# Sixteen copies of value sums issued from ACT's queue, in a windowed attention with two feed-forward layers

## The chip, the cores and the metric

One NeuronCore of a Trainium2 chip runs the whole program in one launch. The metric is the device time in microseconds of that core. Its engines are TensorE (PE, matmuls), VectorE (DVE), ScalarE (ACT), GpSimd (POOL) and SyncE (SP, which only issues DMAs here). Each works through its own instructions in order; semaphores tie them together.

## The reference

Inputs and output are float32. There are 2 batches, 8 heads, 768 positions and a head dimension of 64. The mean of v over 32 positions, `v_sum`, is what the copies in question carry.

```
k_sum = k.reshape(B, H, nb, 32, D).max(axis=3)          # nb = 24 blocks of 32 positions
v_sum = v.reshape(B, H, nb, 32, D).mean(axis=3)
scores_l = scale * q @ k^T, kept where |i - j| < 16, else -1e9
scores_s = scale * q @ k_sum^T + log(32)
a = softmax(concat[scores_l, scores_s])
x = a @ concat[v, v_sum]                                # to 1536 tokens x 512
x = relu(x @ w_in)**2 @ w_out                           # 512 -> 2048 -> 512
h = x @ w2_in; solu = h * softmax(h); out = layernorm(solu) * g_ln @ w2_out
```

## The kernel before

The 1536 tokens are cut into four pieces t of 512, 256, 256 and 512 tokens, each inside one batch. A unit u is one piece and one pair of heads hp (h and h + 4), so there are 16 units, four to a piece. A unit's queries are worked on in blocks of 64, and each block meets 96 positions of k and v, the window of all its queries, and the 24 block sums of its batch, 120 rows in all.

The values of a unit lie in one of three tiles `vw`, 120 rows x 8 blocks x 128 columns (two heads of 64); unit u uses tile u mod 3. `load_v` (lines 258 to 273) fills rows 0 to 95 from memory. Rows 96 to 119 are the 24 sums, the same for every block of the unit. They are made once for each batch and pair of heads: `load_vst` loads v into a tile `kl`, `sum_v0` adds on POOL or DVE, `sum_v1` multiplies with a selector on TensorE, and `sum_v2` copies the result from PSUM to the tile `vs` of the batch, on ACT six times and on DVE twice. `place_vs` (lines 275 to 279) copies them from `vs` to the tile `vw` with one DMA for a unit, repeated over the unit's 8 or 4 blocks: 96 KB for a unit of 512 tokens, 48 KB for one of 256.

The whole order is written out by hand in `ORDER` (lines 21 to 59), a list of steps with a letter, a number and at times an engine (a ACT, d DVE, p POOL); every engine's instructions stand in the order in which the steps emit them. The letters that matter here: lk, lq, lv, ls, l are loads (k, q, v, v for the sums, weights), all issued by SP; k, K and q, Q transpose k and q and copy them from PSUM; y, j, J are the three steps of the sums and P is `place_vs`. For the attention S is scores, R the mask and maximum on DVE, E the exponential on ACT (four activations and four reads), n and N the normalization, T the transposition, C its copy to SBUF (`pt`), V the product with the tile `vw`, H and X the split of its result into a high and a low part on ACT and DVE. a to e, F and f turn the 8-byte weights that were loaded into float32 pairs, a and many F on ACT. M, U, G, D, O are the first feed-forward layer: matmul, relu, two squares on ACT, the low part, and the second matmul. The later layer is emitted after the list.

The stretches of the list around four of the copies:

```
... n6 j3 lk6 k10 K10a k11 K11d N6p l4 J3a P3 m4 F1a f1p T6 m5 lv4 E7 n7 N7p F2a S4 R8 C6a a3 b3 ...
... f5p V5 lv7 H5 P6 Q8d j5 J5d l8 lq10 a6 a7 X5 G1 ls6 T10 C10a lv8 b6 ...
... O8 G9 a13 l14 a14 c12 d12 E19 U10d R20 D9d G10 M11 n19 e12 P12 lv13 P13 N19p U11d lv14 E20 V12 n20 H12 N20p P14 R21 E21 ...
... H14 X14 G13 D13p l16 E23 O12 P15 G14 M15 e14 O13 n23 l17 D14d O14 ...
```

SP issues only DMAs, so its order is the order of the l and P steps, and it stops at each until what that transfer needs is there.

Of the kernel before, what the change touches and what calls it, by code (L numbers as in the profile page):

```python
# [62 lines left out]
def attn_moe_kernel(ctx, tc, q, k, v, w_in, w_out, w2_in, w2_out, g_ln, out):  # L63
    nc = tc.nc
# [4 lines left out]
    P = 128  # L69
# [4 lines left out]
    NSUM = S // 32  # L74
    WK = 96
    WN = WK + NSUM
# [82 lines left out]
    NVB = 3  # L159
    vw = [ap.tile([WN, NBLK, P], F32, name=f"vw{i}") for i in range(NVB)]  # L160
# [114 lines left out]
    def place_vs(u):  # L275
        t, hp = units[u]
        for b, s0, b0, nb in segs[t]:
            src = vs[b][32 * hp:32 * hp + NSUM]
            nc.sync.dma_start(out=vw[u % NVB][WK:WN, b0:b0 + nb], in_=src.unsqueeze(1).to_broadcast([NSUM, nb, P]))

    def prep_kw(u, eng):

# [401 lines left out]
    def load_g(n):  # L684
# [7 lines left out]
        "k": lambda n: prep_k0(n // 2, n % 2), "K": lambda n, e: prep_k1(n // 2, n % 2, COPY[e]), "m": prep_ks,  # L692
        "q": prep_q0, "Q": lambda u, e: prep_q1(u, COPY[e]), "w": lambda u, e: prep_kw(u, COPY[e]),
        "y": lambda i, e: sum_v0(i, ENG[e]), "j": sum_v1, "J": lambda i, e: sum_v2(i, COPY[e]), "P": place_vs,

        "S": att_s, "R": att_r, "E": att_e, "n": att_n0, "N": lambda g, e: att_n(g, ENG[e]), "T": att_t,
# [62 lines left out]
```

## Time and profile before

| | |
|---|---|
| three timed runs | 500.70, 501.98, 502.87 us; median 501.98 |
| profiled execution | 504.72 us, its span 503.0 us |
| busy: PE, DVE, ACT, POOL | 473.9 (94%), 339.0 (67%), 247.9 (49%), 116.9 (23%) us |
| copies of the sums | 16, at 25.2 to 147.3 us, 799 to 977 ns of SP's queue each |
| clock granted to TensorE, mean | 0.983 |

The span runs from the first to the last instruction, and the execution's own time has what lies around it. Busy time counts arithmetic only: an issue of a DMA occupies the queue of the engine that issues it, but is not counted as its busy time. In a timeline a line is the start, the duration, the engine, the line of the kernel, the instruction with the tile written and the tiles read, and in brackets how long the engine was idle before it and what ended that.

### The profile page before, as it was taken

Reading aid. Unit: us, or ns where it says so; the run is one execution under the profiler, and the core shown is the slowest. Engines: PE = TensorE matmul, PEld = TensorE weight load, DVE = VectorE, ACT = ScalarE, POOL = GpSimd, SP = SyncE. Lnnn points to the kernel's source line nnn. Section 1 sums busy time; section 2 is a strip of 40 time slices with the busy share of each in tenths; the row PEclk is TensorE's granted clock in tenths of the full one; section 3 lists DMA queues with packets and bytes.
Section 4 is the critical chain, followed back from the end, with each engine's and each line's share of the span. In section 5 each row is a group of like instructions: output and inputs, shape, how many; then the busy total and the mean of one; then the engine's idle time right before and its main releaser. Section 6 shows DMA issues by size and latency. Waiting matters only on the chain.

```text
span 503.0 us, 8088 instructions
## 1 busy us (share of the span) xinstructions
PE 473.9 (94%) x2968; PEld 394.8 (78%) x2968; DVE 339.0 (67%) x756; ACT 247.9 (49%) x576; POOL 116.9 (23%) x134
## 2 busy tenths in 40 slices
PE   3686699999999999999999999999999999999997
PEld 2465477789999888888888888888877888888886
DVE  4777889875785459345237778986778787665560
ACT  3687688777764544435326536465522332222231
POOL 3255432721321331511022302101312112110000
PEclk9788899999999999999999999999999999999999
DMA  9999886486224122333011332330000010000011
GB/s 189 206 233 201 214 206 171 98 156 137 74 60 110 51 83 87 81 94 81 36 43 42 124 124 89 125 125 1 1 1 1 22 42 22 21 22 22 21 43 42
DMA packets 60359, 44.04 MB, mean 88 GB/s; under 512 B 46624, under 2 KB 49184, under 8 KB 60320
## 3 DMA queue, kind: packets, MB, share of 16 engines
q1 hardware_dynamic: 60320, 43.53, 34.9%
q8 instruction: 23, 0.38, 0.3%
q14 instruction: 16, 0.13, 0.1%
HBM read 39.19 MB, written 3.15 MB: 84 GB/s over the span
## 4 chain that ended last, share of the span: by engine, by line
PE 78%; DVE 7%; DMA 4%; issue 4%; POOL 3%; ACT 3%; SPq 2%; POOLq 0%; DVEq 0%; ACTq 0%
PE h L505 25%; PE acc L537 23%; PE po L647 13%; PE h L587 9%; DMA kl<-in_v_dram 2%; PE lt L624 2%; PE at L316 2%; PE at L381 1%; POOL kl L242 1%; DMA qr<-in_q_dram 1%; PE at L361 1%; DVE sm L337 1%; ACT sm L345 1%; DVE wf L444 1%; POOL sm L355 1%
## 5 line engine op out<-in xcount | busy, mean ns | idle before, releaser
L505 PE MATMUL h<-xh,wi 128*128 128x512 f32 (+1 forms) x432 | 131.9, 371 | 0.0
L537 PE MATMUL acc<-gh,wo 128*128 128x512 f32 (+1 forms) x432 | 130.2, 368 | 0.0
L505 PEld LDWEIGHTS h<-xh,wi 128*128 128x128 f32 x432 | 79.3, 190 | 14.5 <-issue 0.8
L537 PEld LDWEIGHTS acc<-gh,wo 128*128 128x128 f32 x432 | 78.7, 188 | 14.3 <-issue 1.0
L505 PE MATMUL h<-xl,wi 128*128 128x512 f32 (+1 forms) x216 | 79.5, 368 | 0.0
L537 PE MATMUL acc<-gl,wo 128*128 128x512 f32 (+1 forms) x216 | 79.2, 367 | 0.2 <-DVE gl L94 0.2
L587 PE MATMUL h<-w,wf 128*128 128x512 f32 x288 | 67.4, 390 | 0.5 <-DVE st L598 0.5
L587 PEld LDWEIGHTS h<-w,wf 128*128 128x128 f32 x288 | 54.0, 188 | 11.9 <-PE lt L624 0.7
L515 ACT ACTIVATE r<-h 128x512 f32<-128x512 f32 (+1 forms) x34 | 19.0, 559 | 63.7 <-PE h L505 62.6
L94 POOL TENSOR_TENSOR gl<-r,gh 128x512 fp32r<-128x512 f32 (+1 forms) x19 | 21.5, 1131 | 117.9 <-ACT r L524 103.4
L523 ACT ACTIVATE gh<-r 128x512 fp32r<-128x512 f32 (+1 forms) x54 | 31.3, 580 | 35.0 <-DVE r L517 26.8
L537 PEld LDWEIGHTS acc<-gl,wo 128*128 128x128 f32 x216 | 40.7, 188 | 7.1 <-DVE gl L94 0.7
L505 PEld LDWEIGHTS h<-xl,wi 128*128 128x128 f32 x216 | 41.0, 190 | 6.3
L94 DVE TENSOR_TENSOR gl<-r,gh 128x512 fp32r<-128x512 f32 (+1 forms) x35 | 25.8, 738 | 23.6 <-ACT r L524 21.8
L597 ACT ACTIVATE st<-h,nm 128x1024 f32<-128x1024 f32 x12 | 13.4, 1117 | 51.1 <-DVE nm L594 51.1
L454 DVE SCALAR_TENSOR_TENSOR wf<-st,wf 128x512 uint32<-128x512 uint32 x48 | 36.5, 763 | 1.0
L345 ACT ACTIVATE sm<-sm,mn 128x120 f32<-128x120 f32 x96 | 36.5, 383 | 0.5 <-DVE mn L337 0.4
L437 ACT ACTIVATE wf<-st 128x512 f32<-128x512 f32 x48 | 31.1, 660 | 8.9 <-DMA st<-in_moe_w_in_dram 6.4
L451 DVE SCALAR_TENSOR_TENSOR wf<-st,wf 128x512 uint32<-128x512 uint32 x48 | 34.3, 718 | 1.1
L524 ACT ACTIVATE r<-r 128x512 f32<-128x512 f32 (+1 forms) x54 | 31.6, 585 | 1.8
L440 DVE TENSOR_SCALAR wf<-wf 128x512 f32<-128x512 f32 x48 | 24.8, 518 | 11.1 <-ACT wf L437 11.0
L610 POOL TENSOR_TENSOR vr<-vr,mhalf 128x1 f32<-128x1 f32 x12 | 6.6, 550 | 105.0 <-DVE vr L609 105.0
(126 smaller groups left out, 755.6 us busy)
## 6 DMA issues: line engine op xcount, KB each, us to landing
st<-in_moe_w_out_dram SPq DMA_DIRECT2D x24, 512.0 KB, 3.4
st<-in_moe_w_in_dram SPq DMA_DIRECT2D x32, 256.0 KB, 4.2
st<-in_moe_w_in_dram SPq DMA_DIRECT2D x8, 512.0 KB, 4.0
kl<-in_v_dram SPq DMA_DIRECT2D x8, 384.0 KB, 4.2
kl<-in_k_dram SPq DMA_DIRECT2D x16, 192.0 KB, 4.5
out_dram<-ob SPq DMA_DIRECT2D x11, 256.0 KB, 2.0
vw<-in_v_dram SPq DMA_DIRECT2D x16, 168.0 KB, 3.9
qr<-in_q_dram SPq DMA_DIRECT2D x16, 128.0 KB, 5.0
```

The lines of the kernel that those rows point to most:

```text
L94: eng.tensor_tensor(out=lo, in0=x, in1=hi.bitcast(F32), op=ALU.subtract)
L345: nc.scalar.activation(out=sm[:, j], in_=sm[:, j], func=AF.Exp, bias=mn[:, j:j + 1], scale=-1.0, accum_out=su[:, j:j + 1])
L437: nc.scalar.activation(out=wf_t[n], in_=st_t[n].rearrange("p (n t) -> p n t", t=2)[:, :, 1], func=AF.Abs)
L440: nc.vector.tensor_scalar(out=wf_t[n], in0=wf_t[n], scalar1=C_LO, scalar2=C_HI, op0=ALU.max, op1=ALU.min)
L451: nc.vector.scalar_tensor_tensor(out=w, in0=st[:, :, 0], scalar=29, in1=w, op0=ALU.logical_shift_right, op1=ALU.bitwise_or)
L454: nc.vector.scalar_tensor_tensor(out=w, in0=st[:, :, 1], scalar=0xC0000000, in1=w, op0=ALU.bitwise_and, op1=ALU.bitwise_or)
L505: nc.tensor.matmul(ps[:, 0:hi - lo], wi[:, wsel, d, :], x[t][:, d, lo:hi], start=(n == 0), stop=(n == 3 * HP - 1))
L523: nc.scalar.activation(out=gh, in_=r, func=AF.Square)
L524: nc.scalar.activation(out=r, in_=r, func=AF.Square)
L537: nc.tensor.matmul(acc_t[e][:, lo:hi], wo[:, wsel, e, :], x, start=(edge(s, -1, 3) and i == 0), stop=(edge(s, 1, 3) and i == 2))
L587: nc.tensor.matmul(h2[:, fs], x[:, c, :], w_t[NW1 + nh * NDC + c][:, wsel, :], start=(n == 0), stop=(n == 3 * NDC - 1))
L647: nc.tensor.matmul(po[:, ds], x[:, cs], w_t[NW1 + 8 + c][:, wsel, ds], start=(n == 0), stop=(n == 3 * NF2 - 1))
```

## The change

The DMAs of `place_vs` are issued by ACT instead of SP. Their sources, destinations and sizes, and the order in which the steps are emitted, stay as they are, so that on ACT a copy stands between the activations of the steps around it.

```diff
     def place_vs(u):
         t, hp = units[u]
         for b, s0, b0, nb in segs[t]:
             src = vs[b][32 * hp:32 * hp + NSUM]
-            nc.sync.dma_start(out=vw[u % NVB][WK:WN, b0:b0 + nb], in_=src.unsqueeze(1).to_broadcast([NSUM, nb, P]))
+            nc.scalar.dma_start(out=vw[u % NVB][WK:WN, b0:b0 + nb], in_=src.unsqueeze(1).to_broadcast([NSUM, nb, P]))
```

## Rows read from the trace of the kernel before

**Rows 1.** Windows: stretch, its length, busy us of each engine (instructions), clock, DMA, GB/s.
```profile
0.00:62.50 62.50, 39.11 (x426) 29.97 (x426) 46.23 (x165) 39.39 (x130) 26.84 (x52) 0.86 1.03 209
62.50:100.00 37.50, 35.92 (x320) 27.96 (x319) 32.37 (x94) 30.92 (x92) 16.55 (x15) 1.00 0.65 161
100.00:150.00 50.00, 49.83 (x556) 45.17 (x554) 36.08 (x130) 36.60 (x123) 14.43 (x15) 1.00 0.50 104
150.00:503.00 353.00, 349.06 (x1671) 291.72 (x1671) 224.32 (x369) 141.02 (x234) 59.08 (x52) 1.00 0.18 56
```
**Rows 2.** Line 279: its instructions, ns min/median/max, first and last start in us.
```profile
L279 SPq DMA_DIRECT2D vw<-vs x16: 799/852/977, 25.2 to 147.3; - x16
```
**Rows 3.** Timeline of SP's queue from 112 us (P12 and the load behind it).
```profile
112.52 0.84 SPq L279 DMA_DIRECT2D vw<-vs  x1
113.42 0.51 SPq L269 DMA_DIRECT2D vw<-in_v_dram  x1
```
**Rows 4.** Timeline of ACT and PE from 129 us (G10's squares, V12).
```profile
129.18 0.42 ACT L523 ACTIVATE gh<-r 128x256 fp32r<-128x256 f32 x1 [0.43 <-PE acc L537]
129.63 0.42 ACT L524 ACTIVATE r<-r 128x256 f32<-128x256 f32 x1
...
130.51 1.15 PE L381 MATMUL at<-pt,vw 120*64 120x64 f32 x32
```
**Rows 5.** The tile vw: all transfers into it, from issue to landing.
```profile
DMA to landing us min/median/max: 2.0/3.8/5.6
```
**Rows 6.** Windows, columns as in rows 1.
```profile
58.00:60.00 2.00, 2.00 (x11) 1.49 (x5) 1.60 (x11) 0.30 (x1) 0.00 (x0) 0.50 0.89 287
125.00:130.70 5.70, 5.70 (x76) 5.24 (x76) 4.45 (x18) 5.21 (x19) 0.44 (x1) 1.00 0.00 1
```
**Rows 7.** Timeline of ACT from 136 us (H13).
```profile
136.72 0.60 ACT L397 ACTIVATE xh<-at 128x512 fp32r<-128x512 f32 x1 [1.87 <-PE at L381]
```
**Rows 8.** Timeline of ACT, DVE and PE from 147.9 us (G14, D14, O14).
```profile
147.94 0.40 ACT L523 ACTIVATE gh<-r 128x256 fp32r<-128x256 f32 x1
...
148.87 0.98 DVE L94 TENSOR_TENSOR gl<-r,gh 128x256 fp32r<-128x256 f32 x1 [0.43 <-ACT r L524]
...
149.91 0.39 PE L537 MATMUL acc<-gl,wo 128*128 128x256 f32 x1 [0.17 <-DVE gl L94]
```
**Rows 9.** Timeline of ACT, DVE and PE from 44 us (K10, F1, b3, scores).
```profile
44.20 0.49 ACT L679 ACTIVATE kT<-at 128x384 f32<-128x384 f32 x1 [2.34 <-PE at L199]
...
45.01 0.63 ACT L679 ACTIVATE wi<-wf 128x512 fp32r<-128x512 f32 x1
...
48.88 0.46 DVE L440 TENSOR_SCALAR wf<-wf 128x512 f32<-128x512 f32 x1 [0.47 <-ACT wf L437]
...
57.14 1.08 PE L316 MATMUL at<-kw,qT 64*64 64x120 f32 x16 [1.94 <-DVE qT L676]
```
**Rows 10.** Timeline of ACT, DVE and PE from 71 us (H5, b6, T11).
```profile
71.43 0.38 ACT L397 ACTIVATE xh<-at 128x256 fp32r<-128x256 f32 x1 [1.29 <-PE at L381]
...
72.47 0.42 DVE L440 TENSOR_SCALAR wf<-wf 128x512 f32<-128x512 f32 x1
...
77.92 0.62 PE L361 MATMUL at<-ident,sm 128*120 128x128 f32 x4 [0.77 <-DVE sm L355]
```
**Rows 11.** Timeline of PE from 38 us (V1, j3).
```profile
38.09 1.15 PE L381 MATMUL acc<-pt,vw 120*64 120x64 f32 x32 [1.02 <-DMA vw<-vs]
...
43.02 0.40 PE L249 MATMUL acc<-kl,sel 96*24 96x128 f32 x2 [2.95 <-POOL kl L242]
```
**Rows 12.** Chain that ended last: start, duration, what (a load of v, M0, M1).
```profile
32.71 6.72 DMA kl<-in_v_dram
...
58.22 4.07 PE h L505 x12
...
63.60 2.99 PE h L505 x12
```
**Rows 13.** Waits of SP's queue: us in total, times, longest.
```profile
SPq L279 <- ACT vs L679: 7.6, 1, 7.6
```

## The prediction

> **What bounds the kernel now.** I read the table by stages first [rows 1]. In the first 62.5 us TensorE is busy for 39.11 us only: it waits there for the attention's operands, the 16 DMA engines are full (share 1.03), and DVE (46.23) and ACT (39.39) are busier than it is. From 62.5 to 100 us TensorE is busy for 35.92 of 37.50, so 1.6 us are still lost to other engines. After that it is the bound itself: 49.83 of 50.00, then 349.06 of 353.00. So a load that comes earlier can pay only in the first stage, while a delay that reaches TensorE's own order after 62.5 us is paid in full, and nothing behind it gives it back.
>
> Next the sixteen copies. Each holds SP's queue for about 0.85 us (799 to 977 ns) [rows 2]. SP runs ahead of the other engines: P12 was issued at 112.52 us, and SP's next issue began at 113.42, when that one had ended [rows 3]; the products V12, which P12 serves, start 18 us later, at 130.51 [rows 4]. ACT has no such lead. It works through its instructions in the written order, and a copy on its queue leaves when ACT gets there. The question for each copy is therefore where in ACT's order it falls, what stands behind it, and when TensorE wants the tile. The transfers themselves stay the same, on the same 16 engines.
>
> **The change part by part.** It removes 16 x 0.85 = 13.6 us of issue from SP and adds them to ACT, as waiting places of the sequencer and not as work of the engine. No instruction is added. No new wait on TensorE appears either: the products that free a tile are followed on ACT by the H of the same unit before the next P of that tile comes up. I walked through ORDER with ACT's timeline beside it and found four copies with no cover.
>
> P12. In the order stand G10, M11, P12, lv13, P13, E20, V12. G10's first square on ACT is released by TensorE at 129.18, its second starts at 129.63 and ends at 130.05 [rows 4]. P12 comes right after, so it leaves between 129.63 and 130.05; I take 129.84. TensorE does M11 meanwhile and wants V12 at 130.51. Transfers into this tile land 2.0 us after issue at the fastest, 3.8 at the median [rows 5]. From 125 to 130.7 us the DMA engines stand still (share 0.00) [rows 6], so I stay near the fast end and take 2.5. 129.84 + 2.5 - 130.51 = **1.8 us** of TensorE standing still (ends: 129.63 + 2.0 gives 1.1; 130.05 + 3.8 gives 3.3). ACT can't come earlier by running ahead: G10 waits for TensorE itself. P13 behind it and P14 delay E20, E21 and the two pt copies by two to three issues, 1.7 to 2.6 us; TensorE is then 1.8 late itself, and ACT's next idle time (1.87 us before 136.72 [rows 7]) takes the rest.
>
> P15. ACT runs without a gap up to G14 at 147.94; its second square releases DVE's gl at 148.87 after 0.43 us of idling, and that releases TensorE at 149.91 after 0.17 [rows 8]. ACT leads this chain, so P15 ahead of G14 is paid. I take **0.75**, one issue less the tail of the read still running (ends 0, if ACT's arithmetic runs beside an issue, and 0.98).
>
> P3. It follows J3a, whose sums it reads, and stands before F1a at 45.01 [rows 9]. Behind it are E7 and a3; DVE sits idle for 0.47 us until a3 is there, at 48.88, and then DVE's run leads up to qT, for which TensorE waits 1.94 us at 57.14 [rows 9]. So the delay reaches the start of the first M0: **0.85** (ends 0, and 1.7 if it also waits for a load of SP's).
>
> P6. ACT's H5 starts at 71.43, after 1.29 us of idling [rows 10], and a6 follows it. P6 comes between. DVE takes a6's output at 72.47, as soon as it is there or nearly so, and leads this stretch: TensorE waits 0.77 us for DVE's sm at 77.92 [rows 10]. One issue less a little slack is **0.7** (ends 0 and 0.98).
>
> The twelve others I cost at **0.2** together. They have ACT's idle time behind them, as P2 the 2.34 us before 44.20 [rows 9], or delay something that is not wanted for some us. If that cover is gone, each costs up to 0.85; I allow 2 in all. P1 leaves later too, and V1 at 38.09 was already waiting for it; but TensorE then idles for 2.95 us until POOL's sums are there at 43.02 [rows 11], so some 2 us of that are covered.
>
> What SP gives back. A long DMA leg of the chain's front is the load of v at 32.71, 6.72 us [rows 12]. It waits for its buffer, not for SP; but P1's 96 KB no longer stand in the queue before it, and 96 KB at 209 GB/s [rows 1] are 0.47 us. I credit **-0.4** (ends 0 and -1.0, since more loads may move up). The longest wait of SP at the copies, 7.6 us for J6a [rows 13], goes too, but in a stage where TensorE is already full.
>
> Sum: 1.8 + 0.75 + 0.85 + 0.7 + 0.2 - 0.4 = **+3.9 us**. The profiled execution took 504.72 us, of which the span is 503.0; it would be 508.6. The three timed runs have their median at 501.98, 2.7 below it, and the terms do not hang on that difference: 501.98 + 3.9 = **505.9 us**.
>
> The granted clock is a term that I leave at zero and keep for the range. It fell to 0.50, the 1.2 GHz level, in 58 to 60 us [rows 6] after the 1.94 us wait at 57.14 in a stretch where TensorE did little; M0 took 4.07 us there, M1 at full clock 2.99 [rows 12]. The stall at V12 is as long, but lies in dense work. If the clock falls there, add about 1.1.
>
> **The rivals.** (1) An issue on ACT costs it next to nothing, since its arithmetic runs on. For it: the records show SP issuing, never ACT. Against: SP's own next issue starts only when the last has ended [rows 3]. P12 still lands late, so +1.1 to 1.8: 503.5 us.
>
> (2) The issues on ACT are dearer than on SP, since both queues issue at once in the front, where SP issues almost without pause. With twice the price for P3, P4, P6 and the small ones (0.85 more at three places, 2 for the twelve) and the clock falling at V12 (1.1): 3.9 + 2.6 + 2 = 8.5, 510.5 us. The Trainium skill speaks for this one (Perfetto Trace Analysis, DMA Instruction — HWDGE): the block that generates descriptors is shared by the issuing sequencers and locked for one at a time, and the profiled issue contains the wait for the lock. By that an ACT copy in the front pays up to one SP issue more; SP being the only one to issue here, no row of before shows such a wait.
>
> (3) Faster: SP's issue is what holds back the front. P0 to P4 cost its queue 5 x 0.85 = 4.25 us in the front; if every load behind them moved up by that and the operands with them, 4.25 us of TensorE's 23.4 idle us there (62.5 - 39.11) [rows 1] would go. Less a stall at V12 at its low end, 1.1, and with ACT's issues hidden: -3.15, 498.8 us. It decides for faster from the point where the front gains over 1.1. Against it: the DMA share is 1.03 there, so an earlier issue mostly waits longer. The same page (DMA Optimizations) advises to spread DMAs over the queues when descriptor generation is the bottleneck; by the DMA share it is not.
>
> (4) The change does nothing that counts: stalls at V12 and credits of the front cancel, 502 us.
>
> **How the numbers follow.** Mine 0.56, with its own range 503.8 to 509; rivals (1) 0.18, (2) 0.14, (3) 0.08, (4) 0.04. What a measurement can tell from no change is some 0.5%, 2.5 us: slower from 504.5 on. Of mine 0.06 lies below that. Slower 0.50 + 0.14 = 0.64; same 0.06 + 0.18 + 0.04 = 0.28; faster 0.08. The range leaves out rival (3) and the far end of (2): 501.5 to 510.
>
> **What would show it.** P12's issue on ACT after 129.6 us counted from the same G10, and a TensorE wait before V12, released by the copy, of 1.1 to 3.3 us; a wait of 0.8 to 1.1 instead of 0.17 at the gl products after P15; M0 starting 0.4 to 1.7 us later than 58.22; a6 and DVE's use of it later by 0.7.  Wrong would be: V12 without a wait, M0 at 58 or earlier, or arithmetic of ACT's that starts beside a running issue of its own.

## The result, and the profile after

The changed kernel takes 508.24 us (four runs, 507.95 to 509.40), the kernel before beside it 501.71 (four runs, 500.70 to 502.87). The ratio is 1.0130, with a 95% interval of 1.0107 to 1.0154: **6.5 us slower, between 5.4 and 7.7**. Measured again on another occasion it was 507.93 against 502.02, a ratio of 1.0116 (1.0069 to 1.0163). The forecast was 505.9, slower, with a range up to 510: the sign and the range hold, the size was 2.3 us short. A ratio is of fast runs alone, so one run further down, 508.66 us with P1 alone on ACT, counts in its kernel's median and not in its ratio.

The profiled execution took 508.02 us. By stages, with the columns of [rows 1]:

```profile
0.00:62.50 62.50, 40.20 (x422) 31.39 (x423) 45.74 (x163) 39.42 (x129) 26.11 (x52) 0.86 0.97 201
62.50:100.00 37.50, 35.31 (x315) 27.14 (x315) 32.56 (x95) 31.16 (x91) 15.38 (x14) 1.00 0.76 188
100.00:150.00 50.00, 48.17 (x539) 43.42 (x538) 34.74 (x127) 34.57 (x113) 13.95 (x16) 1.00 0.37 82
150.00:506.30 356.30, 352.14 (x1697) 294.66 (x1695) 226.15 (x375) 143.71 (x245) 61.73 (x54) 1.00 0.18 57
```

The third stage has lost 1.7 us of TensorE's work and the last one is longer by what came before it. The span grew by 3.3 us only (503.0 to 506.3), half of what the timed runs lost. The trace of before stands about 3 us above its own timed runs, and the first experiment is about that.

**P12 and V12**, the timelines of ACT and PE that answer to [rows 4]:

```profile
130.59 0.42 ACT L523 ACTIVATE gh<-r 128x256 fp32r<-128x256 f32 x1 [0.42 <-PE acc L537]
131.03 0.42 ACT L524 ACTIVATE r<-r 128x256 f32<-128x256 f32 x1
131.04 1.65 ACTq L279 DMA_DIRECT2D vw<-vs  x2
132.74 0.39 ACT L345 ACTIVATE sm<-sm,mn 128x120 f32<-128x120 f32 x1 [1.29 <-DVE r L517]
...
133.81 1.15 PE L381 MATMUL at<-pt,vw 120*64 120x64 f32 x32 [1.83 <-DMA vw<-vs]
```

P12 leaves just behind the start of G10's second square, V12 waits 1.83 us for it; the granted clock stays at 1.00 through this stage. ACTq marks what ACT's sequencer issues.

**P15 and P6, P3.** First the rows that answer to [rows 8], then those to [rows 10], then P3's.

```profile
149.40 0.42 ACT L524 ACTIVATE r<-r 128x256 f32<-128x256 f32 x1
149.44 0.80 ACTq L279 DMA_DIRECT2D vw<-vs  x1
149.73 0.38 ACT L345 ACTIVATE sm<-sm,mn 128x120 f32<-128x120 f32 x1
...
153.22 0.38 PE L537 MATMUL acc<-gl,wo 128*128 128x256 f32 x1 [0.17 <-DVE gl L94]
```
```profile
72.28 0.38 ACT L397 ACTIVATE xh<-at 128x256 fp32r<-128x256 f32 x1 [0.87 <-PE at L381]
72.34 0.79 ACTq L279 DMA_DIRECT2D vw<-vs  x1
73.18 1.26 ACT L437 ACTIVATE wf<-st 128x512 f32<-128x512 f32 x2 [0.51 <-DMA vw<-in_v_dram]
...
73.89 0.43 DVE L440 TENSOR_SCALAR wf<-wf 128x512 f32<-128x512 f32 x1
...
79.34 0.62 PE L361 MATMUL at<-ident,sm 128*120 128x128 f32 x4 [0.92 <-DVE sm L355]
```
```profile
45.47 0.48 ACT L679 ACTIVATE kT<-at 128x384 f32<-128x384 f32 x1
...
46.27 0.80 ACTq L279 DMA_DIRECT2D vw<-vs  x1
47.11 0.63 ACT L679 ACTIVATE wi<-wf 128x512 fp32r<-128x512 f32 x1 [0.87 <-DVE kT L676]
```

P15's issue at 149.44 runs beside E23's activations, which stand before it in ACT's order and were queued already; the wait at the gl products is 0.17 us as before. P6 lets a6 and so DVE's b6 come 0.57 later than H5 does (73.89 against 72.47 is +1.42; H5 is +0.85). P3 lets F1a begin 2.10 later than at 45.01, of which K10 before it brings 1.27 and P3 the other 0.83.

**The front.** PE's long waits, and the first M0 and M1 in the chain (as [rows 9, 11 and 12]):

```profile
34.45 0.62 PE L249 MATMUL acc<-kl,sel 96*24 96x128 f32 x2 [4.49 <-POOL kl L242]
40.97 1.97 PE L381 MATMUL acc<-pt,vw 120*64 120x64 f32 x32 [2.02 <-DMA vw<-vs]
47.58 0.95 PE L361 MATMUL acc<-ident,sm 128*120 128x128 f32 x4 [2.02 <-POOL sm L355]
...
58.05 1.07 PE L316 MATMUL at<-kw,qT 64*64 64x120 f32 x16 [0.51 <-DVE qT L676]
```
```profile
35.95 4.89 DMA vw<-vs
59.12 4.06 PE h L505 x12
64.50 2.95 PE h L505 x12
```

The first two waits are new in size. Before, the same two matmuls waited 0.75 us and 1.02 us [rows 11 has the second]. The first follows from a load on SP's queue, here in the trace after and, below it, in that of before:

```profile
27.63 0.31 SPq L236 DMA_DIRECT2D kl<-in_v_dram  x1
```
```profile
24.62 0.47 SPq L236 DMA_DIRECT2D kl<-in_v_dram  x1
...
32.28 0.40 PE L249 MATMUL acc<-kl,sel 96*24 96x128 f32 x2 [0.75 <-POOL kl L242]
```

The load is ls2, v for the third set of sums. It issues 3 us later although SP has less to do. The waits of SP's queue say why (over the whole run: us in total, times, longest); before, there was no row of a load that waits for a copy:

```profile
SPq L272 <- DMA vw<-vs: 6.5, 3, 2.8
SPq L190 <- DMA vw<-vs: 4.7, 1, 4.7
SPq L236 <- DMA vw<-vs: 4.4, 1, 4.4
SPq L422 <- DMA vw<-vs: 3.0, 1, 3.0
...
```

With two smaller rows these are 20.0 us, but only 8.1 of them lie before 62.5 us: the 4.4 of L236, which is ls2, 2.8 of L272 and 0.9. The 4.7 and the 3.0 come later. ls2 fills a tile `kl` and has no use for the copy's tile. What it shares with P0 is a semaphore. Each DMA reports its landing on one of eight, DMAHW0 to DMAHW7, given out in turn over the DMAs of both queues, and in these programs a DMA does not issue until the last one on its semaphore has landed. In the built programs (engine, number among all DMAs of the program from 0, line, transfer, waits):

```
before, SP    28 L236 DMA kl<-in_v_dram 96x2x512 [waits DMAHW4_49,PE_49]
before, SP    29 L279 DMA vw_106<-vs 24x8x128 [waits DMAHW5_49,Activation_49]
after,  ACT   21 L279 DMA vw_106<-vs 24x8x128 [waits DMAHW5_49]
after,  SP    29 L236 DMA kl<-in_v_dram 96x2x512 [waits DMAHW5_49,PE_49]
```

Before, P0 stood one place behind ls2. After, it stands eight places ahead of ls2 and so has the same semaphore; but ACT gets to it at 22.55 us only, and by the events of the semaphore it lands at 27.56. ls2 leaves at 27.63.

### The profile page after: what moved, and what is told of

Same layout as the page of the kernel before. It is cut to its first block, busy times and chain, and to the rows that moved or that the text cites. A ratio compares the mean times of both kernels' runs of the same rounds, so it can differ in the third digit from the quotient of the medians.

```text
span 506.3 us, 8090 instructions
## 1 busy us (share of the span) xinstructions
PE 475.8 (94%) x2968; PEld 396.6 (78%) x2968; DVE 339.2 (67%) x756; ACT 248.9 (49%) x576; POOL 117.2 (23%) x134
## 4 chain that ended last, share of the span: by engine, by line
PE 80%; DMA 7%; issue 3%; DVE 3%; ACT 3%; POOL 2%; SPq 1%; ACTq 0%; POOLq 0%; DVEq 0%
PE h L505 25%; PE acc L537 24%; PE po L647 13%; PE h L587 9%; DMA kl<-in_k_dram 2%; DMA qr<-in_q_dram 2%; PE lt L624 2%; PE at L316 2%; DMA vw<-vs 1%; PE at L381 1%; PE at L361 1%; PE acc L361 1%; PE acc L381 1%; DMA kl<-in_v_dram 1%; DVE wf L454 1%
## 5 line engine op out<-in xcount | busy, mean ns | idle before, releaser
L440 DVE TENSOR_SCALAR wf<-wf 128x512 f32<-128x512 f32 x48 | 24.9, 520 | 12.0 <-ACT wf L437 11.8
L355 POOL TENSOR_TENSOR sm<-sm,su 128x480 f32<-128x480 f32 x17 | 17.3, 1017 | 61.2 <-DVE su L351 48.3
```

The source lines that it names most:

```text
L440: nc.vector.tensor_scalar(out=wf_t[n], in0=wf_t[n], scalar1=C_LO, scalar2=C_HI, op0=ALU.max, op1=ALU.min)
```

## The experiments

Theory A: what costs is that the copies are late on ACT, for the products that read them (P12, P1) and for SP's loads that share their semaphores (P0). Theory B: what costs is ACT's time of issue, 0.8 us for each copy behind which ACT waits. Two of the twelve runs are of unchanged kernels; in the others the edit is which units' copies ACT issues, as in

```diff
-            nc.scalar.dma_start(out=vw[u % NVB][WK:WN, b0:b0 + nb], ...
+            (nc.scalar if u in (0,) else nc.sync).dma_start(out=vw[u % NVB][WK:WN, b0:b0 + nb], ...
```

and in some a step moved in ORDER. In one table, with the difference from the kernel before (its median was 501.7 to 502.0 beside them) worked out from the ratio:

| copies on ACT | moved | median us | ratio (95%) | us |
|---|---|---|---|---|
| all (the change) | | 508.24 | 1.0130 (1.0107 to 1.0154) | +6.5 |
| all, again | | 507.93 | 1.0116 (1.0069 to 1.0163) | +5.8 |
| all but P12 | | 506.73 | 1.0083 (1.0059 to 1.0106) | +4.2 |
| all | P12 | 504.95 | 1.0068 (1.0042 to 1.0094) | +3.4 |
| all | P0, P1, P12 | 503.59 | 1.0040 (1.0016 to 1.0064) | +2.0 |
| P5 to P15 | | 503.74 | 1.0037 (1.0017 to 1.0057) | +1.9 |
| P5 to P15 | P12 | 501.80 | 0.9999 (0.9975 to 1.0024) | -0.1 |
| P0 to P4 | | 505.38 | 1.0053 (1.0026 to 1.0081) | +2.7 |
| P1 | | 504.58 | 1.0045 (1.0015 to 1.0075) | +2.3 |
| P0 | | 502.99 | 1.0024 (1.0003 to 1.0045) | +1.2 |
| P0 | P0 | 501.37 | 0.9988 (0.9972 to 1.0003) | -0.6 |
| P0, P1 | P0, P1 | 502.04 | 0.9993 (0.9971 to 1.0014) | -0.4 |

**A second trace of the kernel before** (no edit).

> The kernel before, unchanged, for a second trace: its profiled execution took 504.72 us where its timed runs take 501.7, so a part of what the change costs is hidden between the two traces. Expected by both theories: an execution near 501.7 us, some 3 us shorter than the first one in the stretch before 62.5 us, and equal to it from 150 us to the end.

Missed: 505.19 us, and the front is no shorter. The first stage of this trace, and below it that of the kernel with P0 alone on ACT and early, whose profiled execution took 501.28:

```profile
0.00:62.50 62.50, 39.52 (x424) 30.26 (x424) 46.56 (x165) 39.06 (x129) 26.86 (x52) 0.89 1.06 216
```
```profile
0.00:62.50 62.50, 41.51 (x456) 31.68 (x457) 49.00 (x169) 43.03 (x144) 27.93 (x53) 0.97 1.04 210
```

The 71 timed runs of the kernel before beside the experiments took 499.7 to 504.8 us. Both of its profiled executions stand at the upper end or above. The second kernel, whose timed runs agree with before's, shows in its trace how a shorter front looks: 2 us more of TensorE's work done by 62.5 us, and a granted clock of 0.97 instead of 0.86 to 0.89. The traces also show what goes with a long execution. In both traces of before, POOL's three adds for the sums (L242) run beside two steps of DVE (L440, L444), and the two take 2.13 and 2.22 us; in the trace after, the load that the adds wait for comes later, and the two steps, done by then, take 0.85. First before, then after:

```profile
54.34 2.72 POOL L242 TENSOR_TENSOR kl<-kl 96x512 f32<-96x512 f32 x3
54.58 1.30 DVE L440 TENSOR_SCALAR wf<-wf 128x512 f32<-128x512 f32 x1
55.92 0.83 DVE L444 TENSOR_SCALAR wf<-wf 128x512 uint32<-128x512 uint32 x1
```
```profile
56.69 0.42 DVE L440 TENSOR_SCALAR wf<-wf 128x512 f32<-128x512 f32 x1
...
58.37 2.61 POOL L242 TENSOR_TENSOR kl<-kl 96x512 f32<-96x512 f32 x3 [1.88 <-DMA kl<-in_v_dram]
```

Of the fourteen traces of this case seven have the adds beside the steps, which then take 1.9 to 2.2 us together, and seven do not, with 0.8 to 0.9. The first seven executions took 2.5 to 3.4 us more than the median of their kernel's timed runs, the others between 2.2 less and 1.7 more. So before was profiled twice in the long form. How 1.3 us of DVE become some 3, and how many timed runs have this form, is not shown. The front's loss is taken from timed runs, and the trace after against that of before understates it. The waits of ls2 and V1 below lie before 42 us, ahead of this place.

**P12 alone back on SP.** The edit: `u` in all but 12.

> All copies from ACT's queue but P12, which SP issues again. Both theories: the wait of V12 (1.83 us in the trace after, released by ACT's copy, against 0.17 before) goes, and nothing else: 508.2 - 1.8 = 506.4 us. If the time stays at 508.2, something else is late there and takes the wait's place.

Measured 506.73. V12 has no wait in its trace, and 4.2 of the 6.5 us stay.

**The front on SP, and its mirror.** The edits: `u in (5, ..., 15)`, and `u in (0, 1, 2, 3, 4)`.

> P0 to P4 from SP's queue again, P5 to P15 from ACT's. Theory A (in the front a copy from ACT's queue lands late, and SP's loads and the first value products wait for it: ls2 for P0, V1 for P1): of the 6.5 us lost, V12's 1.8 and some 0.5 of P5 and P6 stay, so 504.0 us. Theory B (what costs is ACT's time, 0.8 us for each copy behind which it waits): P0, P1, P2 and P4 stood beside other waits and only P3's 0.85 us comes back, so 507.4 us.

> The mirror: only P0 to P4 from ACT's queue, the rest from SP's. Theory A: the front's 4 us are all here, 505.7 us. Theory B: only P3's 0.85 us, 502.6 us. If this and the kernel with P0 to P4 on SP both stand near the kernel before, the two parts of the loss are not independent.

503.74 and 505.38. The first is theory A's number and 3.7 us below B's. Its trace shows the one loss that is left (ACT, then PE):

```profile
126.30 1.65 ACTq L279 DMA_DIRECT2D vw<-vs  x2
...
129.07 1.15 PE L381 MATMUL at<-pt,vw 120*64 120x64 f32 x32 [1.83 <-DMA vw<-vs]
```

The mirror's median is A's number too; its ratio says +2.7 us (1.3 to 4.1), so B's 0.8 lies outside the interval, and A's 3.9 inside. In its trace ls2 waits as in the kernel after:

```profile
SPq L236 <- DMA vw<-vs: 4.4, 1, 4.4
```

**P0 alone, at its place and early.** The second moves the step: `... K4a P0 N0p ...` instead of `... R2 P0 E2 ...`.

> Only P0 from ACT's queue, all the rest from SP's. Theory A (the load ls2 on SP's queue waits for the completion semaphore that P0's copy holds until it has landed, 27.56 us in the trace after, and issues 3 us late): the wait of the sums' matmul for ls2 grows from 0.75 to some 4 us, of which later waits take back a part, so 504 us (503 to 505.5). Theory B (ACT's time of issue): P0's 1.4 us stand beside PE's waits for other work, 502 us, no difference from before.

> Only P0 from ACT's queue, and emitted right after K4a instead of after R2: ACT issues it several us earlier, so it has landed before ls2 asks for its semaphore; ACT's time of issue is the same. Theory A: ls2 issues near 24.6 again, 502 us, as before. Theory B: ACT's issue costs what it costs in the kernel with P0 alone, whether that is nothing or something; the two agree within 0.7 us.

502.99 and 501.37: +1.2 us (0.2 to 2.3) and -0.6 (-1.4 to 0.2), for the same issue on the same engine. ACT's P0 and SP's ls2 with P0 at its place, then with P0 early:

```profile
22.62 1.43 ACTq L279 DMA_DIRECT2D vw<-vs  x1
...
27.07 0.31 SPq L236 DMA_DIRECT2D kl<-in_v_dram  x1
```
```profile
18.53 1.44 ACTq L279 DMA_DIRECT2D vw<-vs  x1
...
24.95 0.47 SPq L236 DMA_DIRECT2D kl<-in_v_dram  x1
```

In the first, SP's waits have 2.6 us of ls2 for a copy; by the events of their semaphore P0 lands at 27.00, and ls2 leaves at 27.07. With P0 4 us earlier ls2 leaves 2.1 us sooner, near the 24.62 of the kernel before, and no load waits more than 0.6 us for a copy. The place of P0 decides, not its issue alone.

**P12 early, and P0, P1 and P12 early, all on ACT.** The moves: `C17a P12 T18`, `K4a P0 N0p`, `C1a P1 n2`.

> All sixteen copies from ACT's queue, P12 emitted right after C17a, some 5 us earlier on ACT. Both theories: V12's wait of 1.83 us goes and the front is as in the kernel after, 506.4 us. If 0.8 us of issue ahead of Q14's or G9's arithmetic is then on the path, up to 507.2.

> All sixteen from ACT's queue, with P0 emitted after K4a, P1 after C1a and P12 after C17a; as many issues on ACT as in the kernel after. Theory A (the copies' lateness is the loss): 503.3 us, what is left being P5, P6 and a part of P2 to P4. Theory B (the issues' time is the loss): only V12's wait goes, 506.4 us.

504.95 and 503.59. The first is 1.5 below what both expected, and V12 has no wait in its trace; the difference from the kernel after, 2.4 to 3.1 us by the two ratios, holds V12's 1.9 within the intervals. The second is A's number: all sixteen are issued by ACT as in the change, and 3.8 to 4.5 of its 5.8 to 6.5 us are gone. What is left of it, 2.0 us, is put to the front by elimination: P5 to P15 with P12 early cost -0.1 us (below). In the trace ls2 leaves at 26.29 (SP, then PE; V1 at 38.76 has no wait):

```profile
26.29 0.47 SPq L236 DMA_DIRECT2D kl<-in_v_dram  x1
...
34.16 0.40 PE L249 MATMUL acc<-kl,sel 96*24 96x128 f32 x2 [3.16 <-POOL kl L242]
...
38.76 1.15 PE L381 MATMUL acc<-pt,vw 120*64 120x64 f32 x32
```

P0 and P1 early cost nothing when they alone are on ACT (-0.4, below), so the 2.0 us point at P2 to P4, or at all five coming together. P2 to P4 were not timed by themselves; this part stays open.

**The change again.** No edit.

> The changed kernel, unchanged, beside the other three on one chip. All theories: 508.2 us. The kernel with P12 emitted earlier came out at 504.95 where 506.4 was expected; if the changed kernel is itself nearer to 507 here, V12's wait explains that difference alone.

507.93 (505.69 to 510.38), no nearer to 507. The 1.1 us by which the move of P12 gained more than V12's wait are within the intervals and not explained further.

**P1 alone, and P0 and P1 early.** The edits: `u in (1,)`; `u in (0, 1)` with the moves of P0 and P1.

> Only P1 from ACT's queue, at its place (ACT issues it behind K8a and a2, near 36 us, where SP issued it at 31.5). Theory A: V1's wait, 1.0 us in the trace before, grows to some 2 to 4 us and an SP load 8 places behind P1 is held until it has landed; later waits take back a part: 503 us (502 to 504.5). Theory B (ACT's time of issue): 0.8 us beside V1's wait, 501.8 us, no difference from before.

> P0 and P1 from ACT's queue, emitted right after K4a and after C1a, all the rest from SP's. Theory A: both have landed before V0, V1 or a load of SP's asks for them, so V1's wait of 1.0 us goes, and what the next wait takes back of it is open: 501.4 us (500.5 to 502). Theory B: two issues of 1.4 and 0.8 us on ACT where it was busier, 502.5 us. If ls2 or the key loads still wait for a copy, the time is near the one of P0 alone at its old place, 503.

504.58 and 502.04: +2.3 us (0.8 to 3.8) for P1 at its place, theory A's number above the top of its range; nothing (-1.5 to 0.7) for both early. P1's issue on ACT and V1 on PE, with P1 at its place; then with P1 early:

```profile
34.18 1.41 ACTq L279 DMA_DIRECT2D vw<-vs  x1
...
41.15 1.12 PE L381 MATMUL acc<-pt,vw 120*64 120x64 f32 x16 [4.10 <-DMA vw<-vs]
```
```profile
27.30 0.79 ACTq L279 DMA_DIRECT2D vw<-vs  x1
...
36.55 1.15 PE L381 MATMUL acc<-pt,vw 120*64 120x64 f32 x32
```

In the first, the chain has the transfer with 6.83 us, in a front whose DMA engines are full, and 2.7 us of lateness (34.18 against 31.49, when SP issued it) turn into a wait longer by 3.1. With P1 early the wait is gone, but the time is that of the kernel before: the 1.02 us that V1 waited there [rows 11] were no loss. Nor were 2.4 us for which a load of v (L272) waits for a copy in this trace.

**P5 to P15 on ACT, P12 early.** The edit of the front on SP, and `C17a P12 T18`.

> P5 to P15 from ACT's queue, P0 to P4 from SP's, P12 emitted right after C17a. With P12 at its old place this took 503.7 us and its trace showed a loss at V12 alone. Theory A: eleven issues on ACT cost nothing where their copies are in time, 501.8 us. Theory B: some 0.2 us an issue stay, 503 us.

501.80, a ratio of 0.9999. Eleven issues on ACT cost nothing that can be measured here: -0.1 us (-1.3 to 1.2). Nor do the 12.4 us for which SP's loads wait for these copies. V12 has no wait in this trace, with P12 out six us before it:

```profile
123.66 0.79 ACTq L279 DMA_DIRECT2D vw<-vs  x1
...
129.85 1.15 PE L381 MATMUL at<-pt,vw 120*64 120x64 f32 x32
```

By theory B some 1.2 us should have stayed; its 503 lies just inside the interval's end, and A's 501.8 in its middle. The difference to the same kernel with P12 at its old place, 1.9 us, is P12's price by itself.

## Why the prediction came out as it did

Right in sign and inside its range, and one term of it right to a tenth; the rest of its sum was made of the wrong terms. That it fell only 2.3 us short is partly luck: the 2.3 us put on P15, P3 and P6, of which little is to be seen, stood in for a front that was put at next to nothing and cost 2.7 us by itself.

**P12: right.** Forecast +1.8; V12 waits 1.83 us in the trace, and the timed pair with P12 late and early differs by 1.9. The way was right too: ACT could not run ahead of G10, and the copy landed 2.64 us after its issue, where 2.5 was taken. The clock did not fall at that wait.

**P15, forecast +0.75: wrong, no cost is seen.** The end "0, if ACT's arithmetic runs beside an issue" is what came. What waits for an issue is what stands behind the copy in ACT's order. The sequencer reached P15 while E23's four activations were queued ahead of it, and the issue ran beside them. The sign named for a wrong forecast, arithmetic beside a running issue, is in the trace. Where what comes next stands behind the copy, ACT stands still for the whole issue, as at E20, which starts at 132.74 when P12 and P13 have been issued.

**P3, forecast +0.85, and P6, +0.7.** As delays they are there, 0.83 us at F1a and 0.57 at b6. As losses little is to be seen. M0 is 0.90 later (59.12 against 58.22), inside the 0.4 to 1.7 that were asked for, but by chance: F1a was 2.10 us late, 1.27 of it from before P3, and DVE gave 1.28 back on the way, because POOL's adds ran beside its two steps in the trace of before only. So M0's own wait shrank from 1.94 to 0.51, and the 1.94 of [rows 9] belong to the long form of the execution. Past P6, TensorE's lateness against the trace of before grows from 1.27 to 1.42 us. P6 alone was not timed; P5 to P15 without P12's lateness cost -0.1 (-1.3 to 1.2), which leaves it small room.

**The twelve others, forecast 0.2, and SP's relief, -0.4: the step that failed.** They hold P0 and P1, which cost +1.2 and +2.3 us each by itself, and P0 to P4 together +2.7. For P1 the step said that some 2 us of V1's longer wait are covered by the 2.95 us of idling behind it. That wait grew by 3.1 us with P1 alone on ACT, and the cover took up half of it: the sums' matmul behind V1 is 1.5 us late there (44.52 against 43.02). But the transposition after it, which waits for POOL's sm as in the trace after (2.02 us at 47.58), is 3.2 late again (47.76 against 44.60), so the cover did not hold. P0 has no word of its own in the step. V0 does not wait for it; what waited was ls2, a load on SP's queue, by the shared semaphore. So SP's first loads did not move up, as the credit of -0.4 had it, but back: in the front they wait 8.1 us for copies. "The transfers themselves stay the same" was true, and left out that each is also the next one's permission to start.

By timed pieces: 2.7 for P0 to P4 and 1.9 for P12 are 4.6 us of the 5.8 to 6.5. Within the front the pieces do not add up (P0 and P1 by themselves are more than all five, and P2 to P4 were not timed), so how the 2.7 divide among the five is open. The rest, 1 to 2 us, is within the intervals of the pieces and is not settled. The granted clock may hold some of it. The mean granted clock of the changed kernel was 0.982 to 0.983 in all eight runs, that of the kernel before 0.988 on average over the 71 (0.979 to 0.997), and over those 71 runs the time falls by 0.11 us for each 0.001. This would be 0.6 us, but a stretch at the 1.2 GHz level and the wait before it come together, and no run here tells which brought which.

**The rivals.** (1), an issue that is hidden and P12 alone, has the mechanism right for P5 to P15 (503.5 forecast; that kernel took 503.74) and not for the front. (2) has 510.5 by dearer issues, in a sum that names 1.1 us for the clock and leaves it out (with it 511.6). The issues on ACT took 790 ns at the median, less than SP's 852.

```profile
L279 ACTq DMA_DIRECT2D vw<-vs x16: 789/790/1410, 22.5 to 149.4; - x16
```

In the trace after, the fifteen ACT issues behind the first took 0.789 to 0.825 us, at most 0.825 with an issue of SP's running beside them and at most 0.821 without; the first, 1.41, is as long where no issue of SP's ran beside it (1.40 at 60.39 with P5 to P15 on ACT). The lock on descriptor generation that the Trainium skill tells of (Perfetto Trace Analysis, DMA Instruction — HWDGE) would show as ACT issues that grow while SP issues; no run here shows it at work. (3), SP's relief, did not come in any kernel: the best ratio is 0.9988 (0.9972 to 1.0003). Nor did (4), a front that gives back what V12 loses: the front lost as well. No version tried beats the kernel before.

## What to carry to other kernels

Before moving a DMA to another queue, note three times for it: when the new engine reaches it in its written order, when its reader wants it, and what it would hold if it lands late. The last one includes the other queue: where completion semaphores are handed out in turn, the DMA eight places on waits for this one, whatever it carries. The engine's time of issue is the small part, since only what stands behind the copy waits for it, and moving three steps further up in the order gave back most of the loss here.

## What was not expected of the hardware and its programs

- A DMA queue can hold another: SP's loads waited up to 4.7 us for copies from ACT's queue, loads of k, of v for the sums and of weights among them, which share no tile with the copies. That is the program's semaphores at work, not the DMA engines. Such a wait is not a loss by itself: 12.4 us of them cost nothing with P5 to P15 on ACT, while 2.6 us of ls2 for P0 went with +1.2 us.
- The first DMA that ACT issued took 1.39 to 1.44 us in all twelve traces that have one, whichever it was (P0 at 22.55, P1 at 34.18 where it was alone, P5 at 60.39 where it was first); all others some 0.8.
- ACT's sequencer issues a DMA while activations that were queued ahead of it still run (149.44 beside 149.73 above), so that copy, behind a backlog, cost its engine nothing.
- Two steps of DVE that take 0.85 us together took 1.9 to 2.2 in the seven traces in which POOL's adds ran beside them. Where they did not meet, the adds had in five traces of seven waited 1.8 to 2.6 us for their load of v and so came behind the steps; why DVE is slower beside them is not shown.
